# First phase of an attention and feed-forward block: second half of a projection by pairs of row tiles, V and weights ahead of K's DMA transposes

## The chip, the cores and the metric

One core of one Trainium2 chip. The metric is device time in microseconds (us) of one execution. The record also has each execution's mean granted TensorE clock (1.000 is full speed). In the profile's lines PE is TensorE, PEld its weight loads, DVE VectorE, ACT ScalarE, POOL GpSimd and SPq the DMA issues of SyncE.

## The reference

```python
x   = A_x                                             # (1, 2048, 1024), bf16
mod = silu(c) @ w_mod                                 # six vectors sa, ca, ga, sb, cb, gb
h   = layernorm(x) * (1 + ca) + sa
q   = h @ wq                                          # 32 heads of 128
p   = softmax(q @ k.T / sqrt(128)); o = p @ v         # 4 kv heads, the last 512 keys
x   = x + ga * (o @ wo)
h   = layernorm(x) * (1 + cb) + sb
x   = x + gb * ((silu(h @ w_gate) * (h @ w_up)) @ w_down)   # inner size 3584
```

## The kernel before

The kernel walks through four chunks of 512 rows. In the steady part each step is one head: scores (`s_ps`), the query product of a head seven steps ahead (`q_ps`), and the weighted sum (`o_ps`). Only the first phase, up to about 36 us, is touched. There the layernorm of the first chunk is multiplied by `1 + ca` (`hs`), and the query products of heads 0 to 6 ("D") are accumulated over eight row tiles `dt` of the weights, which come in four DMAs `wq8` of two row tiles each. The shift `sa` is added later as a bias: `sa_mm` computes it in one-column products, `sh_mm` multiplies it with the weights.

The DMA queue (all issued by SyncE, in this order):

```python
    for tt in range(QT):            # four 128-row tiles of x
        load_x(tt)
    for half in range(DH):
        load_wm(1, half)            # w_mod columns of ca
        load_wq8(2 * half)          # heads 0-7, two row tiles each
        load_wq8(2 * half + 1)
    load_wm(0, 0)                   # w_mod columns of sa, first half
    h10 = hpool.tile([P, DT, TCW], BF16, name="hT", tag="hT")
    load_wm(0, 1)
    kT = blkB("kT", [P, Hkv, W])
    for kv in range(Hkv):           # K, transposed on the way in
        pin(nc.sync.dma_start_transpose(
            out=kT[:, kv, :], in_=A_k_cache[0, kv, k0:k0 + W, :]), "dma")
    ...
    for kv in range(Hkv):
        load(v_sb[:, kv, :, 0:Dh], v_v[:, kv])
    load_wq(0, 2)                   # third group's weights: heads 8-11, two DMAs of 512 KB
```

The part of PE's order that is touched (program order is kept here):

```python
    def q0(g, dts, src=None):       # head g, row tiles dts: one 128x512 product each
        for dt in dts:
            nc.tensor.matmul(q0_ps[g], lhsT=w0(g, dt), rhs=..., start=(dt == 0), stop=(dt == DT - 1))
    ...                             # first half of D: row tiles 0 to 3 of all seven heads
    for g in range(3):
        q0(g, range(4, DT))
    q0(3, (4, 5))
    sa_mm(0, (0, 1))
    q0(3, (6, 7))
    sa_mm(0, (2, 3))
    sa_out(0)                       # DVE: PSUM -> sa, sa_bf
    q0(4, (4, 5))
    sh_mm(0, range(4))
    q0(4, (6, 7))
    sh_mm(0, range(4, H0))
    for dt in range(4):
        ln_mod(("h1", 0), dt, ca1, sa)                                   # DVE
    nc.vector.tensor_copy(out=bias_q, in_=one_ps[:, 1, 0:H0])            # DVE
    q0(5, (4, 5))
    sa_mm(1, (0, 1))                # writes one_ps: waits for that copy
    q0(5, (6, 7))
    sa_mm(1, (2, 3))
    sa_out(1)
    q0(6, (4, 5))
    sh_mm(1, range(H0))             # waits for sa_bf
    q0(6, (6, 7))
    ...
    nc.vector.tensor_tensor(out=bias_q, in0=one_ps[:, 2, 0:H0], in1=bias_q, op=ALU.add)
    q0_ps[H0] = mm("q_ps")          # takes one_ps's bank: waits for that addition
    q0(H0, range(DT), h10)          # head 7
```

After this come head 0's scores (they need K of kv head 0, "K0"), head 8's query product (the third group's weights) and head 0's weighted sum (V of kv head 0, "V0").

Of the kernel before, what the change touches and what calls it, by code (L numbers as in the profile page):

```python
# [11 lines left out]
BF16 = mybir.dt.bfloat16  # L12
# [576 lines left out]
def fast_path(ctx, tc, flag, A_x, A_k_cache, A_v_cache, A_wq, A_wo, B_x, B_w_gate, B_w_up,  # L589
# [4 lines left out]
    P = 128  # L594
    _, S, D = A_x.shape
    _, Hkv, Sk, Dh = A_k_cache.shape
# [9 lines left out]
    DT = D // P  # L606
    FT = F // P
    WT = W // P
# [20 lines left out]
    const = ctx.enter_context(tc.tile_pool(name="const", bufs=1))  # L629
# [13 lines left out]
    def blkB(name, shape, dt=BF16):  # L643
        return pb_.tile(shape, dt, name=name, tag="B")
# [4 lines left out]
    def mm(name, shape=(P, 512), dt=FP32):  # L649
        return psp.tile(list(shape), dt, name=name, tag="mm", bufs=4)  # L650
# [9 lines left out]
    def pin(ins, what="steps"):  # L660
        return tc.keep_in_program_order(ins) if stage[what] else ins

    def fetch(out, in_):
        pin(nc.sync.dma_start(out=out, in_=in_), "dma")  # L664

    def load(out, in_):
        with nc.allow_non_contiguous_dma(reason="weight slice"):
            fetch(out=out, in_=in_)
# [32 lines left out]
    def load_wq(cc, hg, parts=(0, 1)):  # L701
        for i in parts:
            t = blkB("wq", [P, 4, 512])
            load(t, wq_v[:, 4 * i:4 * i + 4, hg * 512:(hg + 1) * 512])
            wq_tiles[(cc, hg, i)] = t

    H0 = 7
# [14 lines left out]
    h10 = hpool.tile([P, DT, TCW], BF16, name="hT", tag="hT")  # L722
    load_wm(0, 1)
    kT = blkB("kT", [P, Hkv, W])
    for kv in range(Hkv):
        pin(nc.sync.dma_start_transpose(  # L726
            out=kT[:, kv, :], in_=A_k_cache[0, kv, k0:k0 + W, :]), "dma")
    VN = Dh + 2
    v_sb = const.tile([P, Hkv, WT, Dh + 32], BF16, name="v_sb")
    for kv in range(Hkv):  # L730
        load(v_sb[:, kv, :, 0:Dh], v_v[:, kv])
    load_wq(0, 2)

    ones_bf = const.tile([P, P], BF16, name="ones_bf")
    nc.vector.memset(ones_bf, 1.0)
# [24 lines left out]
    nc.gpsimd.tensor_tensor(out=sil_r, in0=c_r, in1=ec, op=ALU.mult)  # L760
    nc.gpsimd.memset(v_sb[:, :, :, Dh:VN], 1.0)
    siluc = const.tile([P, DT], BF16, name="siluc")
# [229 lines left out]
    def h_scale(dt, src=None, on_act=False):  # L992
        src = h10[:, dt, :] if src is None else src
        if on_act:
            nc.scalar.activation(out=hs[dt // 4][:, dt % 4, :], in_=src, func=ACT.Identity,
                                 scale=ca1[:, dt:dt + 1])
        else:
            nc.vector.tensor_scalar(out=hs[dt // 4][:, dt % 4, :], in0=src,
                                    scalar1=ca1[:, dt:dt + 1], scalar2=None, op0=ALU.mult)
# [15 lines left out]
    def w0(g, dt):  # L1015
        return wq8[dt // 2][:, dt % 2, g * P:(g + 1) * P]

    def q0(g, dts, src=None):
        for dt in dts:
            nc.tensor.matmul(q0_ps[g], lhsT=w0(g, dt),  # L1020
                             rhs=hs[dt // 4][:, dt % 4, :] if src is None else src[:, dt, :],
                             start=(dt == 0), stop=(dt == DT - 1))
# [4 lines left out]
    def sh_mm(half, heads):  # L1027
        for g in heads:
            for i in range(4):
                dt = 4 * half + i  # L1030
                nc.tensor.matmul(one_ps[:, 1 + half, g:g + 1], lhsT=w0(g, dt),
                                 rhs=sa_bf[:, dt:dt + 1], start=(i == 0), stop=(i == 3))

    def sa_mm(half, tiles):
        for i in tiles:
            c = 4 * half + i
            for dt in range(DT):
                nc.tensor.matmul(one_ps[:, 0, c:c + 1],
                                 lhsT=wm_tiles[(0, half)][:, dt, i * P:(i + 1) * P],
                                 rhs=siluc[:, dt:dt + 1], start=(dt == 0), stop=(dt == DT - 1))  # L1040

    def sa_out(half):
        c = slice(4 * half, 4 * half + 4)
        nc.vector.tensor_copy(out=sa[:, c], in_=one_ps[:, 0, c])
        nc.vector.tensor_copy(out=sa_bf[:, c], in_=sa[:, c])
# [4 lines left out]
    for i in range(2):  # L1050
# [4 lines left out]
        if i == 0:  # L1055
            mod_cols(1, 1, ca1, True)
            for dt in range(4, DT):
                h_scale(dt)
    for g in range(3):
        q0(g, range(4, DT))  # L1060

    q0(3, (4, 5))
    sa_mm(0, (0, 1))
    q0(3, (6, 7))
    sa_mm(0, (2, 3))
    sa_out(0)
    q0(4, (4, 5))
    sh_mm(0, range(4))
    q0(4, (6, 7))
    sh_mm(0, range(4, H0))  # L1070
    for dt in range(4):
        ln_mod(("h1", 0), dt, ca1, sa)
    nc.vector.tensor_copy(out=bias_q, in_=one_ps[:, 1, 0:H0])
    q0(5, (4, 5))
    sa_mm(1, (0, 1))
    q0(5, (6, 7))
    sa_mm(1, (2, 3))
    sa_out(1)
    q0(6, (4, 5))
    sh_mm(1, range(H0))  # L1080
    q0(6, (6, 7))
    for dt in (4, 5):
        ln_mod(("h1", 0), dt, ca1, sa)
    for dt in (6, 7):
# [119 lines left out]
    def emit_o(g):  # L1204
# [4 lines left out]
        for t in range(QT):  # L1209
            if o_slot["n"] == 0:  # L1210
                o_slot["ps"] = mm("o_ps", (P, SLOTS, VN))
            s_ = o_slot["n"]
            for j in range(WT):
                nc.tensor.matmul(o_slot["ps"][:, s_, :], lhsT=pT[g][:, j, t * P:(t + 1) * P],  # L1214
                                 rhs=v_sb[:, kv, j, 0:VN], start=(j == 0),
                                 stop=(j == WT - 1))
# [146 lines left out]
    for k in range(NU + 1):  # L1363
        if k % 4 >= 2 and 4 * (k // 4) + 12 < NU:
            g = 4 * (k // 4) + 12
# [49 lines left out]
def kernel(tc, *args):  # L1415
    nc = tc.nc
    with tc.tile_pool(name="guard", bufs=1) as gp:
        flag = gp.tile([1, 1], I32, name="flag")
        over = fast_path(tc, flag, *args)
        with tc.If(over > 0):  # L1420
            general_path(tc, *args)
# [30 lines left out]
```

## Time and profile before

| | before |
|---|---|
| median, 6 executions | 1274.25 us (1273.68 to 1274.90) |
| span of the profiled execution | 1272.4 us, mean clock 1.000 |
| first score product starts | 30.48 us |
| first product of the weighted sum (`o_ps`) starts | 35.42 us |
| from there to the end | 1236.96 us |

Busy time by engine, kernel before: busy us, share of the span, instructions.

```profile
PE 1255.9 (99%) x7445; PEld 640.0 (50%) x7587; DVE 610.0 (48%) x1335; ACT 335.6 (26%) x440; POOL 1.3 (0%) x10
```

TensorE bounds the kernel, and from 36 us to the end the list of waits of PE is empty. What is left is the start. PE's waits from 0 to 60 us, kernel before (us in total, times, longest us):

```profile
PE warm_ps L746 <- DVE warm_w L737: 1.6, 1, 1.6
PE q_ps L1171 <- DMA wq<-in_A_wq_dram: 1.1, 2, 0.8
PE q_ps L1020 <- DMA wq<-in_A_wq_dram: 0.5, 1, 0.5
PE h_ps L948 <- DVE xn L852: 0.5, 2, 0.3
PE one_ps L1038 <- DMA wm<-in_w_mod_dram: 0.2, 1, 0.2
```

`q_ps L1171` is head 8's query product: it waited 1.1 us for the third group's weights. `q_ps L1020` is D: it waited 0.5 us for the last `wq8`. The timeline of PE, kernel before (start us, duration us, engine, line, operation, count, idle before and what ended it):

```profile
19.39 2.76 PE L1020 MATMUL q_ps<-hs,wq 128*128 128x512 bf16 x12 [0.54 <-DMA wq<-in_A_wq_dram]
22.39 0.55 PE L1038 MATMUL one_ps<-siluc,wm 128*128 128x1 bf16 x16 [0.24 <-DMA wm<-in_w_mod_dram]
...
25.79 0.54 PE L1038 MATMUL one_ps<-siluc,wm 128*128 128x1 bf16 x16
26.41 0.38 PE L1020 MATMUL q_ps<-hs,wq 128*128 128x512 bf16 x1
26.63 0.54 PE L1038 MATMUL one_ps<-siluc,wm 128*128 128x1 bf16 x16
27.03 0.59 PE L1020 MATMUL q_ps<-hs,wq 128*128 128x512 bf16 x2
27.62 0.84 PE L1031 MATMUL one_ps<-sa_bf,wq 128*128 128x1 bf16 x28
28.33 0.59 PE L1020 MATMUL q_ps<-hs,wq 128*128 128x512 bf16 x2
28.75 1.89 PE L1020 MATMUL q_ps<-hT,wq 128*128 128x512 bf16 x7
30.48 1.03 PE L1182 MATMUL s_ps<-qT,kT 128*128 128x512 bf16 x4
32.30 0.82 PE L1171 MATMUL q_ps<-hT,wq 128*128 128x512 bf16 x3 [0.79 <-DMA wq<-in_A_wq_dram]
...
34.12 0.39 PE L1171 MATMUL q_ps<-hT,wq 128*128 128x512 bf16 x1 [0.35 <-DMA wq<-in_A_wq_dram]
...
35.42 1.07 PE L1214 MATMUL o_ps<-v_sb,pT 128*128 128x130 bf16 x16
```

The durations of neighbours overlap (the pair at 28.33 us is shown with 0.59 us, the next product starts at 28.75), so the starts are what to read. A few records are missing (the pair before 26.63 shows as x1, head 7's eight products as x7). The DMA queue behind it, SyncE's timeline, kernel before:

```profile
14.83 10.23 SPq L726 DMA_TRANSPOSE kT<-in_A_k_cache_dram  x4
25.11 2.92 SPq L664 DMA_DIRECT2D v_sb<-in_A_v_cache_dram  x4
28.07 1.55 SPq L664 DMA_DIRECT2D wq<-in_A_wq_dram  x2
```

The issues of the four transposes and of V stand in front, so the weights are only issued at 28.07. And the table by stretch, kernel before; the column after POOL is the granted clock:

```profile
26.00:29.40 3.40, 3.27 (x65) 2.17 (x64) 1.84 (x7) 1.94 (x3) 0.00 (x0) 1.00 0.92 196
29.40:32.80 3.40, 2.61 (x13) 1.05 (x12) 3.28 (x6) 2.42 (x4) 0.00 (x0) 1.00 0.85 277
```

### The profile page before, as it was taken

Reading aid. Unit: us, or ns where it says so; the run is one execution under the profiler, and the core shown is the slowest. Engines: PE = TensorE matmul, PEld = TensorE weight load, DVE = VectorE, ACT = ScalarE, POOL = GpSimd, SP = SyncE. Lnnn points to the kernel's source line nnn. Section 1 sums busy time; section 2 is a strip of 40 time slices with the busy share of each in tenths; the row PEclk is TensorE's granted clock in tenths of the full one; section 3 lists DMA queues with packets and bytes.
Section 4 is the critical chain, followed back from the end, with each engine's and each line's share of the span. In section 5 each row is a group of like instructions: output and inputs, shape, how many; then the busy total and the mean of one; then the engine's idle time right before and its main releaser. Section 6 shows DMA issues by size and latency. Waiting matters only on the chain.

```text
span 1272.4 us, 18018 instructions
## 1 busy us (share of the span) xinstructions
PE 1255.9 (99%) x7445; PEld 640.0 (50%) x7587; DVE 610.0 (48%) x1335; ACT 335.6 (26%) x440; POOL 1.3 (0%) x10
## 2 busy tenths in 40 slices
PE   8999999999999999999999999999999999999998
PEld 4555555555555555555554444444444444444444
DVE  5666658885778665567564631321122112221122
ACT  3643334343333433334341111011100111011100
POOL 0000000000000000000000000000000000000000
PEclk9999999999999999999999999999999999999999
DMA  9897656778556655454575379336633565425702
GB/s 286 202 252 172 181 141 147 187 161 214 130 141 171 152 134 157 113 154 108 125 199 149 129 222 258 95 93 210 211 110 112 167 211 184 157 91 169 245 18 68
DMA packets 306844, 204.46 MB, mean 161 GB/s; under 512 B 145601, under 2 KB 303297, under 8 KB 306754
## 3 DMA queue, kind: packets, MB, share of 16 engines
q1 hardware_dynamic: 301842, 199.03, 57.0%
q10 hardware_dynamic: 4912, 4.20, 1.0%
q8 instruction: 61, 1.00, 0.3%
q14 instruction: 29, 0.24, 0.1%
HBM read 165.94 MB, written 4.21 MB: 134 GB/s over the span
## 4 chain that ended last, share of the span: by engine, by line
PE 95%; SPq 2%; DVE 1%; issue 1%; DMA 0%
PE gu_ps L1328 30%; PE a_ps L1246 17%; PE q_ps L1171 16%; PE d_ps L1348 15%; PE o_ps L1214 9%; PE s_ps L1182 8%; SPq L664 1%; SPq L726 1%; DMA wq<-in_A_wq_dram 0%; DVE junk L1105 0%; DVE st L833 0%; DVE junk L804 0%; DVE oq L1201 0%; DVE qT L934 0%; DVE f L1259 0%
## 5 line engine op out<-in xcount | busy, mean ns | idle before, releaser
L1184 ACT ACTIVATE pT<-s_ps 128x1024 bf16<-128x1024 f32 x256 | 249.3, 1020 | 346.1 <-PE s_ps L1182 225.5
L1246 PE MATMUL a_ps<-wo,oT 128*128 128x512 bf16 x987 | 240.1, 380 | 1.9
L1171 PE MATMUL q_ps<-hT,wq 128*128 128x512 bf16 x958 | 227.1, 380 | 1.2 <-DMA wq<-in_A_wq_dram 1.1
L1334 DVE TENSOR_TENSOR guT<-gu_ps,sg 128x512 bf16<-128x512 f32 x112 | 77.5, 692 | 287.0 <-ACT sg L1333 287.0
L1328 PE MATMUL gu_ps<-hT,wg 128*128 128x512 bf16 x879 | 210.1, 380 | 0.9
L1333 ACT ACTIVATE sg<-gu_ps 128x512 bf16<-128x512 f32 x112 | 66.9, 597 | 488.7 <-PE gu_ps L1328 417.4
L1348 PE MATMUL d_ps<-wd,guT 128*128 128x512 bf16 (+2 forms) x935 | 193.3, 367 | 0.9
L1328 PE MATMUL gu_ps<-hT,wu 128*128 128x512 bf16 x656 | 161.7, 379 | 0.8
L1246 PEld LDWEIGHTS <-oT 128*128 128x128 bf16 x1024 | 100.0, 98 | 120.7
L934 DVE CAST qT<-q_ps 128x512 bf16<-128x512 f32 x121 | 83.6, 691 | 153.0 <-PE q_ps L1171 150.6
L1171 PEld LDWEIGHTS <-wq 128*128 128x128 bf16 x960 | 93.7, 98 | 114.9 <-DMA wq<-in_A_wq_dram 2.1
L1348 PEld LDWEIGHTS <-guT 128*128 128x128 bf16 x952 | 90.7, 98 | 103.1
L1214 PEld LDWEIGHTS <-pT 128*128 128x128 bf16 x2048 | 126.5, 98 | 30.6 <-issue 0.4
L1328 PEld LDWEIGHTS <-wg 128*128 128x128 bf16 x896 | 87.5, 98 | 105.6
L1214 PE MATMUL o_ps<-v_sb,pT 128*128 128x130 bf16 x2048 | 137.1, 221 | 0.2
L1182 PE MATMUL s_ps<-qT,kT 128*128 128x512 bf16 x469 | 129.4, 380 | 2.3
L1328 PEld LDWEIGHTS <-wu 128*128 128x128 bf16 x672 | 65.7, 98 | 79.4
L1201 DVE TENSOR_TENSOR oq<-o_ps,rl 128x256 bf16<-128x256 f32 (+2 forms) x256 | 100.4, 419 | 3.9
L1352 DVE TENSOR_TENSOR f<-d_ps,gb_bc 128x512 f32<-128x512 f32 (+2 forms) x34 | 22.4, 660 | 140.7 <-PE d_ps L1348 122.1
L1182 PEld LDWEIGHTS <-kT 128*128 128x128 bf16 x512 | 44.9, 98 | 30.8
L1254 DVE TENSOR_TENSOR acc<-a_ps,acc 128x512 f32<-128x512 f32 x64 | 44.0, 688 | 32.6 <-PE a_ps L1246 32.6
L1328 PE MATMUL gu_ps<-hT,v_sb 128*128 128x512 bf16 x219 | 56.8, 380 | 0.3
(97 smaller groups left out, 424.3 us busy)
## 6 DMA issues: line engine op xcount, KB each, us to landing
wq<-in_A_wq_dram SPq DMA_DIRECT2D x64, 512.0 KB
wo<-in_A_wo_dram SPq DMA_DIRECT2D x64, 512.0 KB
wg<-in_B_w_gate_dram SPq DMA_DIRECT2D x56, 512.0 KB
wd<-in_B_w_down_dram SPq DMA_DIRECT2D x56, 512.0 KB
wu<-in_B_w_up_dram SPq DMA_DIRECT2D x42, 512.0 KB
v_sb<-in_B_w_up_dram SPq DMA_DIRECT2D x14, 512.0 KB
x<-in_A_x_dram SPq DMA_DIRECT2D x16, 256.0 KB
wm<-in_w_mod_dram SPq DMA_DIRECT2D x4, 1024.0 KB
```

The source lines that it names most:

```text
L934: nc.vector.tensor_copy(out=t, in_=q_ps)
L1171: nc.tensor.matmul(q_ps, lhsT=w, rhs=hT[("h1", cc)][:, dt, :], start=(dt == 0), stop=(dt == DT - 1))
L1182: nc.tensor.matmul(s_ps[:, i, :], lhsT=kT[:, kv, j * P:(j + 1) * P], rhs=qT[g], start=True, stop=True)
L1184: nc.scalar.activation(out=p[:, 2 * jj:2 * jj + 2, :], in_=s_ps, func=ACT.Exp, scale=scale)
L1201: nc.vector.tensor_tensor(out=dst, in0=ps[:, s0:s0 + cnt, 0:Dh], in1=sc, op=ALU.mult)
L1214: nc.tensor.matmul(o_slot["ps"][:, s_, :], lhsT=pT[g][:, j, t * P:(t + 1) * P], rhs=v_sb[:, kv, j, 0:VN], start=(j == 0), stop=(j == WT - 1))
L1246: nc.tensor.matmul(a_ps, lhsT=oT[(cc, 2 * q + i)][:, hh % 4, t * P:(t + 1) * P], rhs=wo_tiles[(cc, q, dh, i)][:, hh % 4, :], start=(hh == ...
L1254: nc.vector.tensor_tensor(out=acc[(cc, t)][:, dsl], in0=a_ps, in1=acc[(cc, t)][:, dsl], op=ALU.add)
L1328: nc.tensor.matmul(ps[:, n, :], lhsT=gu_w[(cc, fg, nm, dt // 4)][:, dt % 4, fi * P:(fi + 1) * P], rhs=hT[("h2", cc)][:, dt, :], start=(dt ...
L1333: nc.scalar.activation(out=g, in_=ps[:, 0, :], func=ACT.Silu)
L1334: nc.vector.tensor_tensor(out=guT[(cc, fg)][:, fi, :], in0=ps[:, 1, :], in1=g, op=ALU.mult)
L1348: nc.tensor.matmul(d_ps, lhsT=guT[(cc, f // 4)][:, f % 4, t * P:(t + 1) * P], rhs=wd_tiles[(cc, dh, f // 4)][:, f % 4, c0:c0 + w], start=( ...
```

## The change

Two intents. First, no product of D should wait for the last `wq8`: all heads take the third `wq8` (row tiles 4, 5) before any takes the fourth (6, 7). Second, head 8 should not wait for its weights: V0 and the third group's weights are issued ahead of K. No instruction is added or removed.

```diff
     load_wm(0, 1)
     kT = blkB("kT", [P, Hkv, W])
-    for kv in range(Hkv):
+
+    def load_kT(kv):
         pin(nc.sync.dma_start_transpose(
             out=kT[:, kv, :], in_=A_k_cache[0, kv, k0:k0 + W, :]), "dma")
-    ...
-    for kv in range(Hkv):
+
+    def load_v(kv):
         load(v_sb[:, kv, :, 0:Dh], v_v[:, kv])
+
+    load_v(0)
     load_wq(0, 2)
+    load_kT(0)
+    for kv in range(1, Hkv):
+        load_kT(kv)
+    for kv in range(1, Hkv):
+        load_v(kv)
@@
-    for g in range(3):
-        q0(g, range(4, DT))
-
-    q0(3, (4, 5))
+    for g in range(H0):
+        q0(g, (4, 5))
+
+    q0(0, (6, 7))
+    q0(1, (6, 7))
     sa_mm(0, (0, 1))
-    q0(3, (6, 7))
+    q0(2, (6, 7))
     sa_mm(0, (2, 3))
     sa_out(0)
-    q0(4, (4, 5))
+    q0(3, (6, 7))
     sh_mm(0, range(4))
     q0(4, (6, 7))
     sh_mm(0, range(4, H0))
     ...
-    q0(5, (4, 5))
     sa_mm(1, (0, 1))
     q0(5, (6, 7))
     sa_mm(1, (2, 3))
     sa_out(1)
-    q0(6, (4, 5))
+    q0(6, (6, 7))
     sh_mm(1, range(H0))
-    q0(6, (6, 7))
```

More of the change, by code (lines that the diff above doesn't have):

```diff
@@ L724, in fast_path @@
     kT = blkB("kT", [P, Hkv, W])
-    for kv in range(Hkv):
+    VN = Dh + 2
+    v_sb = const.tile([P, Hkv, WT, Dh + 32], BF16, name="v_sb")
+    def load_kT(kv):
         pin(nc.sync.dma_start_transpose(
             out=kT[:, kv, :], in_=A_k_cache[0, kv, k0:k0 + W, :]), "dma")
-    VN = Dh + 2
-    v_sb = const.tile([P, Hkv, WT, Dh + 32], BF16, name="v_sb")
-    for kv in range(Hkv):
+    def load_v(kv):
         load(v_sb[:, kv, :, 0:Dh], v_v[:, kv])
+    load_v(0)
     load_wq(0, 2)
+    load_kT(0)
[3 more added lines that the diff above has]
+        load_v(kv)
     ones_bf = const.tile([P, P], BF16, name="ones_bf")
```

## The prediction

> **What bounds the kernel.** TensorE. The busy table gives PE 1255.9 us of the 1272.4 us span (99%), granted clock 1.00; the list of waits shows none of PE from 36 us to the end. A steady step takes 3.49 us on the timeline. The change touches only the first 36 us and is worth what PE's chain there gets shorter; 2% is out of reach. Upper bound, from the list of waits to 60 us: PE idle for DMA 1.1 us (head 8's query product, third group's weights: 0.79 and 0.35), 0.5 us (second half of D, last wq8 tile), 0.2 us (sa product, its w_mod half): 1.9 us.
>
> **What the change does.** Nothing is added or removed; only PE's order (28 products of D's second half) and the DMA queue's order change.
>
> 1. *D by pairs of row tiles.* Before, PE runs 8+2 products from 16.54 us, waits for the last wq8 tile (last engine 19.34), resumes at 19.39, and waits until 22.39 for the w_mod half of sa that lands at 22.34. After, 14 products need only the third tile (there at 18.0): the 0.5 us wait goes, and 18 instead of 14 of the 28 are done by 22.15. But sa still starts at 22.39: its DMA is ahead of every moved one. The four products won (4 x 0.215 = 0.86 us) are missing later, where they filled waits for DVE:
>  - sa's second half waits until DVE has copied bias_q (25.54 to 25.71, behind 1.38 us of scalings). Before, q0(5)'s pair filled that and it started at 25.79; after, idle about 0.4 us, start 25.75.
>  - Head 7's product takes one_ps's bank and waits for the bias_q addition (28.50 to 28.67). Before, q0(6)'s last pair filled that; it started at 28.75. After, idle about 0.35 us, start 28.7.
>  So the reordering gives 0 to 0.1 us.
>
> 2. *V0 and weights ahead of K.* [...] the trace's completion counts agree (25.24 w_mod, 25.7 K0, 27.2 K3, then V, weights 32.25 and 34.07). Moved ahead, the weights land at 27 to 28.7: the 0.79 and 0.35 us waits go. ACT's exponentials (1.94 us a head) then gate the second head's scores: from first score product to first o product I count 3.7 us instead of 4.94 (30.48 to 35.42). Gain about 1.2 us, kept to the end.
>
> 3. *Cost.* 1.18 MB now precedes K0. At the 0.36 MB/us of the window table (before 20 us), plus about 0.6 us for V0's small packets, that is 3.5 us: K0 lands at about 29.2 (estimate), needed at 30.3. If one DMA engine lags by 1 us, as several landings show, it just misses; I subtract 0.15 us on average. Other K and V parts are needed later.
>
> **Predicted:** gain 1.1 us, 1273.0 us (1271.9 to 1274.2). Faster by over 2%: 0.5%; within 2%: 99%; slower: 0.5%.
>
> **What would show it.** Right: no PE wait on weights near 32 to 34 us; first o product at 34.2 us, not 35.4; first score product still at 30.2 to 30.5; new PE gaps of about 0.4 us near 25.4 and 28.4, released by DVE; sa still at 22.4. Wrong on 1: first score product by 29.7. Wrong on 3: PE waiting for K's transpose before it.
>
> **What would make it wrong.** K0 after 30.3 us (each us late is a us lost); sa's w_mod landing at another time; the spread of runs, 1.2 us over three, as large as the effect.

In the trace of before the loads landed in the order of their issue (last of 16 engines: w_mod 25.24 us, K0 25.71, V0 29.07, the weights 32.25 and 34.07; K3's last but one 27.2). 0 to 0.1 us of point 1 and 1.2 of point 2, less 0.15 of point 3, are the 1.1 us predicted. In point 3, the 0.6 us for V0 is the author's estimate; in the trace of before the four V loads came 0.63 us apart on average (first of 16 engines: 27.67 to 29.56 us). The lag of one engine is measured there too: 16 engines had landed the third `wq8` at 18.00 us, 15 of them at 17.02.

## More of the kernel before

A wide product here is one of 512 columns, against the one-column products of `sa_mm` and `sh_mm`.

## The result, and the profile after

The changed kernel took 1274.53 us (median of 6, 1273.60 to 1275.43) against 1274.25 before; the ratio is 1.0002, with a 95% interval of 0.9989 to 1.0015. A ratio is the mean time of one kernel's runs over that of the other's of the same rounds, so it is not quite the ratio of the medians quoted. The predicted 1273.0 (a gain of 1.1 us) is outside the measurement: nothing was gained. An effect of 1 us is 0.08%, smaller than the interval of any single comparison here, so what follows rests on the traces, on counts of executions, and on differences between kernels that shared the same runs of before.

PE's waits from 0 to 60 us, changed kernel (its lines from L735 on are 8 or 9 higher):

```profile
PE warm_ps L755 <- DVE warm_w L746: 1.6, 1, 1.6
PE h_ps L957 <- DVE xn L861: 1.5, 2, 1.4
PE q_ps L1029 <- DVE bias_q L1094: 0.3, 1, 0.3
PE one_ps L1047 <- DVE bias_q L1083: 0.3, 1, 0.3
```

The waits for DMA are gone, all 1.9 us of them (0.2 us of it, for sa's w_mod half, only because PE came later: that DMA landed at 22.00 us, and sa started at 22.86). The two waits for DVE that the prediction foresaw are there. One wait grew that the change does not touch: the first transposes of x (`h_ps`) waited 1.4 us, because x landed later in this execution. The timeline of PE, changed kernel:

```profile
17.25 5.77 PE L1029 MATMUL q_ps<-hs,wq 128*128 128x512 bf16 x26
22.86 0.54 PE L1047 MATMUL one_ps<-siluc,wm 128*128 128x1 bf16 x16
...
26.22 0.54 PE L1047 MATMUL one_ps<-siluc,wm 128*128 128x1 bf16 x16 [0.26 <-DVE bias_q L1083]
26.62 0.59 PE L1029 MATMUL q_ps<-hs,wq 128*128 128x512 bf16 x2
27.05 0.54 PE L1047 MATMUL one_ps<-siluc,wm 128*128 128x1 bf16 x16
27.45 0.59 PE L1029 MATMUL q_ps<-hs,wq 128*128 128x512 bf16 x2
28.05 0.84 PE L1040 MATMUL one_ps<-sa_bf,wq 128*128 128x1 bf16 x28
29.14 3.33 PE L1029 MATMUL q_ps<-hT,wq 128*128 128x512 bf16 x8 [0.26 <-DVE bias_q L1094]
32.26 1.32 PE L1190 MATMUL s_ps<-qT,kT 128*128 128x512 bf16 x4
...
36.25 1.07 PE L1222 MATMUL o_ps<-v_sb,pT 128*128 128x130 bf16 x16
```

The phase ends at 36.25 us instead of 35.42, 0.83 us later, and from there to the end both kernels take the same (1236.89 and 1236.96 us). So the whole difference is in these lines. The line to stop at is 29.14: head 7's eight products took 3.33 us, where seven took 1.89 before. The table by stretch, changed kernel, says why:

```profile
26.00:29.40 3.40, 2.92 (x66) 2.09 (x66) 1.58 (x7) 1.51 (x3) 0.00 (x0) 1.00 1.96 159
29.40:32.80 3.40, 3.40 (x10) 1.23 (x9) 3.40 (x6) 1.15 (x3) 0.00 (x0) 0.50 1.01 187
```

For one stretch TensorE was granted half its clock. PE looks fully busy there (3.40 of 3.40 us, 10 products) and does less (an execution of this order at clock 1.00, r6 below, has 15 products in 3.38 us): the busy share hides a slow clock. The trace's own records put the stretch at 29.43 to 32.84 us, 3.41 us long. By my estimate from these two numbers, half of that, 1.7 us, is lost if TensorE has work all through it; r6 measured 1.70 us.

The moved DMAs, SyncE's timeline, changed kernel:

```profile
14.90 4.10 SPq L664 DMA_DIRECT2D v_sb<-in_A_v_cache_dram  x1
19.04 2.92 SPq L664 DMA_DIRECT2D wq<-in_A_wq_dram  x2
22.01 6.64 SPq L729 DMA_TRANSPOSE kT<-in_A_k_cache_dram  x4
```

By the completion counts in the trace (last of 16 engines), the weights landed at 27.10 and 28.50 us instead of 32.25 and 34.07, and K0 at 30.38 instead of 25.71.

Three theories, then. **C (clock)**: the changed order leaves so few wide products between the sparse one-column ones that the clock is halved in part of the executions, for 1.7 us. **K (K's landing)**: K0, now behind 1.18 MB, takes the gain. **J or N (start, chance)**: the start jitters with the landing of the first x rows, and the rest is chance; the halved clock has nothing to do with the change.

### The profile page after: what moved, and what is told of

Read it like the earlier page. It is cut to its first block, busy times and chain, and to the rows that moved or that the text cites. A ratio compares the mean times of both kernels' runs of the same rounds, so it can differ in the third digit from the quotient of the medians.

```text
span 1273.1 us, 18160 instructions
## 1 busy us (share of the span) xinstructions
PE 1264.5 (99%) x7587; PEld 641.5 (50%) x7587; DVE 610.1 (48%) x1335; ACT 335.6 (26%) x440; POOL 1.3 (0%) x10
## 4 chain that ended last, share of the span: by engine, by line
PE 97%; DVE 2%; DMA 0%; SPq 0%; issue 0%
PE gu_ps L1336 30%; PE a_ps L1254 17%; PE q_ps L1179 16%; PE d_ps L1356 15%; PE o_ps L1222 9%; PE s_ps L1190 8%; PE q_ps L1029 1%; DVE st L842 0%; DMA x<-in_A_x_dram 0%; DVE junk L1113 0%; DVE junk L813 0%; DVE oq L1209 0%; DVE qT L943 0%; DVE f L1267 0%; DVE f L1266 0%; DVE x L1269 0%
```

## The experiments

r1 to r4 shared one chip and nine runs of before, r5 to r8 a second chip and nine, r9 and r10 a third and nine. "Difference" is the mean of five executions less the mean of those nine; its standard error, from the two spreads, is 0.2 to 0.45 us. By the formal interval of the ratio (about 0.0013 either way) all but r7 hold 1. All results were correct.

| run | mean us | difference | mean clock of the five executions |
|---|---|---|---|
| r1 the change again | 1274.07 | -0.32 | 0.998 0.999 0.999 1.000 0.998 |
| r2 queue order only | 1273.60 | -0.80 | 0.999 0.999 0.999 1.000 0.999 |
| r3 pair order only | 1274.41 | +0.02 | 1.000 0.998 0.999 0.999 0.999 |
| r4 pairs held back | 1273.29 | -1.11 | 0.999 0.999 0.999 1.000 0.999 |
| r5 before, with tail | 1274.99 | +0.51 | 1.000 1.000 1.000 1.000 1.000 |
| r6 change, with tail | 1275.21 | +0.73 | 1.000 1.000 0.999 0.999 0.999 |
| r7 sparser, with tail | 1276.38 | +1.90 | 0.999 0.999 0.997 0.999 0.997 |
| r8 held back, K0 first | 1273.19 | -1.29 | 0.999 1.000 0.999 0.999 1.000 |
| r9 held back, with tail | 1273.99 | -0.17 | 1.000 1.000 1.000 1.000 1.000 |
| r10 early pairs, K0 first | 1272.96 | -1.20 | 1.000 0.999 1.000 0.999 1.000 |

### r1: the change again

No edit.

> The changed kernel, unaltered, for more executions. Theory C (clock): the pair order leaves TensorE so thinly used between about 26 and 29.4 us that in part of the executions the granted clock is halved for one stretch of 3.4 us, at head 7's product and the first scores, which costs about 1.6 us; the rest of the executions gain about 1.1 us or a little less. Then the executions fall in two groups, mean clock 0.998 (slow group) and 0.999 to 1.000, about 1.4 us apart, with at least a fifth in each. Theory K (K's landing): K0 lands at about 30.4 us in every execution and takes the gain by itself; then no difference between groups of clock. Theory N (nothing gained, only the start jitters): executions without the halved clock are on average no faster than those of before.

Measured: 0.3 us faster than before, executions from 1273.26 to 1275.02. Two of five had clock 0.998, the slowest two (1275.02 and 1274.49); the other three averaged 1273.62. That looks as C has it. But this run's profile corrected me on the reading of the clock: its halved stretch was at 8.55 to 11.96 us, after a wait of 2.0 us for x, where the change does nothing. A mean clock of an execution can't tell that stretch from one at 29 us. In its trace the products of that stretch are longer (eight `h_ps` 0.93 us, against 0.62 in the kernel before). Worse, TensorE is idle at the end (4.8 us in before's profile, from 1267.54 to 1272.38), and the clock is recorded as halved there too, where no product is left to slow (in before's profile from 1272.37 us on, in r2's from 1269.97), so 0.999 can mean a harmless tail. Nor do these 0.998 show C, since the one that was profiled came from the start. This called for the tail of r5 to r7.

### r2: only the queue's order

Against before; PE's order is not touched:

```diff
-    for kv in range(Hkv):
-        pin(nc.sync.dma_start_transpose(... kT[:, kv, :] ...), "dma")
-    for kv in range(Hkv):
-        load(v_sb[:, kv, :, 0:Dh], v_v[:, kv])
+    load_v(0)
     load_wq(0, 2)
+    load_kT(0)
+    for kv in range(1, Hkv):
+        load_kT(kv)
+    for kv in range(1, Hkv):
+        load_v(kv)
```

> Only the DMA queue's order of the change; PE's order as before. Theory C: the gain is all here, because the stretch from 26 to 29.4 us stays as dense as before: the waits for the third group's weights are gone, first o product 1.0 to 1.3 us sooner after the first x row tile's product than before, mean clock 1.000 or 0.9995 in nearly all executions, 0.7 to 1.2 us faster than before. Theory K: K0 lands at 30.2 to 30.5 and PE waits 0.3 us or more for it; faster by at most 0.5 us. Theory N: within 0.3 us of before.

Measured: 0.80 us faster; no execution at 0.998. In its trace K0 landed at 30.84 us and PE waited for it; the first score product started at 30.88, and the first `o_ps` 3.71 us later. PE's waits, r2:

```profile
PE s_ps L1191 <- DMA kT<-in_A_k_cache_dram: 0.3, 1, 0.3
PE one_ps L1047 <- DMA wm<-in_w_mod_dram: 0.2, 1, 0.2
```

Both C and K get a part: the queue's order alone gains most of what was predicted, and K0 takes 0.3 us of it, as in my third step, where I had estimated 29.2 us for K0 and subtracted 0.15. K expected at most 0.5 us of gain, so it is not the main cause.

### r3: only the pair order

Against before; the queue is not touched, and the rest of the change's second hunk follows in the same way:

```diff
-    for g in range(3):
-        q0(g, range(4, DT))
-
-    q0(3, (4, 5))
+    for g in range(H0):
+        q0(g, (4, 5))
+
+    q0(0, (6, 7))
+    q0(1, (6, 7))
     sa_mm(0, (0, 1))
 ...
```

> Only PE's pair order of the change; the DMA queue as before. By my recorded step 1 the first score product starts within 0.1 us of before's, and the waits for the third group's weights (0.8 and 0.35 us) stay or grow, so without a halved clock equal to before within 0.2 us. Theory C: a part of the executions, as large as in the changed kernel, has the halved clock (mean 0.998) and is slower by 0.5 to 1.6 us, part of it hidden by the wait for weights; on average 0.3 to 0.8 us slower than before. Rival: the halved clock comes from the queue's order or from chance; then it is as rare here as in before.

Measured: no difference (+0.02 us), one of five at 0.998. C had said 0.3 to 0.8 us slower: a miss in size. The trace shows room for hiding: the third group's weights land at 32.20 and 33.62 us here and head 8 still waits for them (its weight loads waited 1.0 us, in two waits), so time lost before about 32 us is partly made up by a shorter wait. That this is the reason is argued, not shown.

### r4: two pairs held back

Against the change:

```diff
-    for g in range(H0):
+    for g in (0, 1, 2, 3, 4, 6):
         q0(g, (4, 5))
@@
     nc.vector.tensor_copy(out=bias_q, in_=one_ps[:, 1, 0:H0])
+    q0(5, (4, 5))
     sa_mm(1, (0, 1))
@@
-    q0(6, (6, 7))
     sh_mm(1, range(H0))
+    q0(6, (6, 7))
```

> The changed kernel, but q0(5)'s first pair is held back to where PE waits for the copy of bias_q, and q0(6)'s last pair to where it waits for the bias addition: the same products, the gaps filled as before. Theory C: the halved clock is gone or as rare as in the queue-order-only kernel, 0.7 to 1.2 us faster than before, no PE wait of 0.26 us for DVE. If the clock is halved as often as in the changed kernel, the gaps are not its cause. My step 1: the first score product starts at the same time as in the changed kernel's executions of full clock, within 0.1 us, since the held-back pairs only fill waits.

Measured: 1.11 us faster, and the slowest of its five executions (1273.53) was faster than the fastest of before's nine (1273.76). It differs from the change (-0.32 in the same rounds) only in where two pairs of products stand. The timeline of PE, r4:

```profile
27.52 0.84 PE L1040 MATMUL one_ps<-sa_bf,wq 128*128 128x1 bf16 x28 [0.46 <-DVE sa_bf L1054]
28.22 0.59 PE L1029 MATMUL q_ps<-hs,wq 128*128 128x512 bf16 x2
28.65 1.89 PE L1029 MATMUL q_ps<-hT,wq 128*128 128x512 bf16 x8
30.80 1.04 PE L1191 MATMUL s_ps<-qT,kT 128*128 128x512 bf16 x4 [0.26 <-DMA kT<-in_A_k_cache_dram]
```

The waits for bias_q are filled, one of 0.46 us for sa_bf is new (I had overlooked that q0(6)'s first pair stood there), and head 7's eight products take 1.89 us. K0 is waited for here as well. The expectation that the first score product starts within 0.1 us of the change's at full clock can't be read: it started at 30.80, in r6 at 31.11, after different starts of x.

### r5, r6, r7: counting halved stretches

To make the mean clock readable, 20 dummy products keep TensorE busy to the end, so only halved stretches at the start should count: by the 1.7 us estimated above one stretch is 1.7 of 1272 us, so 0.999; two are 0.997. r5 is before with this tail, r6 the change with it, and r7 a sparser version of the change with it:

```diff
+    tail_ps = mm("tail_ps")
+    for _ in range(20):
+        nc.tensor.matmul(tail_ps, lhsT=ones_bf, rhs=warm_w, start=True, stop=True)
     assert not tasks
@@ r7 only, against the change
     q0(1, (6, 7))
+    q0(5, (6, 7))
+    q0(6, (6, 7))
     sa_mm(0, (0, 1))
@@
     sa_mm(1, (0, 1))
-    q0(5, (6, 7))
     sa_mm(1, (2, 3))
     sa_out(1)
-    q0(6, (6, 7))
```

> The kernel before, with 20 dummy products behind its last one (they fill TensorE's idle 4.3 us at the end, so that the mean granted clock of an execution counts only stretches of half clock at the start: 1.000 none, 0.999 one, 0.997 two). An instrument, not a candidate; its time should be that of before within 0.3 us. Theory C (clock halved because of the sparse stretch left by the pair order): at most one of six executions at 0.999. Theory J (the start of the first products jitters by up to 1.7 us with the landing of the x rows; in before the landing of the third group's weights at about 34 us hides that, in the changed kernel nothing does, and the clock is chance): as many half-clock executions as in the changed kernel; its times spread by less than those of the changed kernel.

Measured: no halved stretch in five, the idle end included (all five 1.000; that end is 4.8 us in before's trace, not 4.3). The tail itself costs about 0.5 us (more than the 0.3 I had allowed; standard error 0.33), so r5, r6, r7 and r9 are compared with each other. One of the five took 1276.04 us at full clock, 1.0 us over the next, which nothing on record explains (see r6 for what 1.000 can miss); without it r5's mean is 1274.72.

> The changed kernel with the same 20 dummy products at its end. Theory C: two to four of six executions at 0.999 (5 of the 11 so far showed 0.998, with an idle tail), these at least 0.8 us slower than the ones at 1.000, and the ones at 1.000 about 1.0 us faster than before. Theory J: no more half-clock executions than in the kernel before with this tail; times at 1.000 spread over more than 1 us.

Measured: three of five executions had a halved stretch. They took 1275.73, 1275.81 and 1276.12 us; the two at full clock took 1274.01 and 1274.36. The groups do not overlap and their means are 1.70 us apart, which is half of 3.41 us. At full clock the change is 0.8 us faster than r5 (1274.19, of two executions, against 1274.99; 0.5 us without r5's slowest). The profiled execution was one at full clock: head 7's eight products took 1.89 us. But its trace holds no clock record at all, nor does r9's, so a mean of 1.000 says only that no half clock was recorded. The table by stretch, r6:

```profile
26.00:29.40 3.40, 2.81 (x66) 2.05 (x65) 1.51 (x7) 1.44 (x3) 0.00 (x0) 1.00 2.10 202
29.40:32.80 3.40, 3.38 (x15) 1.29 (x14) 3.40 (x6) 2.27 (x5) 0.00 (x0) 1.00 0.99 99
```

There the first score product started at 31.11 and the first `o_ps` at 34.82, 3.71 us apart as predicted.

> The changed kernel with the last pairs of q0(5) and q0(6) moved up in front of the first sa product, so that no wide product runs between about 26 and 29.3 us; with the same tail. The two pairs delay the sa product by about 0.6 us. Theory C: more half-clock executions than in the changed kernel, at least four of six, and at least 1 us slower on average than the changed kernel. If the halved clock has another cause than the sparse stretch: no more of them than in the changed kernel, and about 0.6 us slower.

Measured: all five had a halved stretch, two of them two (where the second lay is not recorded); 1.17 us slower than r6. The sa product started at 23.72 instead of 22.93 in r6 (0.8 us later, 0.6 expected). The table by stretch, r7, whose halved stretch the trace records at 29.69 to 33.10 us:

```profile
26.00:29.40 3.40, 2.60 (x78) 2.16 (x75) 1.97 (x9) 1.09 (x2) 0.00 (x0) 1.00 1.45 203
29.40:32.80 3.40, 3.01 (x7) 1.12 (x8) 3.37 (x6) 1.57 (x3) 0.00 (x0) 0.54 1.46 146
```

Fewer wide products between 26 and 29.4 us, more halved stretches: 0 of 5, 3 of 5, 5 of 5. J (as many in r5 as in r6) falls, by r5 against r7 above all: 0 against 3 of five alone could be chance.

### r8: K0 first

Against r4:

```diff
-    load_v(0)
-    load_wq(0, 2)
     load_kT(0)
+    load_wq(0, 2)
+    load_v(0)
```

> A candidate: pairs held back as in r4, and in the DMA queue K0 first, then the third group's weights, then V0, the rest of K and V. In r2 and r4 PE waited 0.26 us for K0, which landed at 30.8. Theory K (K0's landing after the moved weights takes part of the gain): K0 lands at about 25.7, the wait is gone, weights land at 29 to 30.5 without a new wait, and the kernel is 0.2 to 0.4 us faster than r4's distance to before, so 1.3 to 1.5 us faster than before. If the weights now arrive after about 31.5 us, a wait for them comes back and the gain is that of r4 or less.

Measured: K0 landed at 25.12 us, the weights at 26.59 and 28.16, no wait for any of them in the list; 1.29 us faster than before against r4's 1.11. The wait of 0.26 us is gone for certain; that it shows as 0.2 us in the time is within the error of the two differences.

### r9: the cure, counted

r4's kernel with r5's tail, no other edit.

> r4's kernel (the change, with q0(5)'s first and q0(6)'s last pair held back) with the 20 dummy products at its end, so that its mean clock counts half-clock stretches as in r5, r6 and r7 (0 of 5, 3 of 5, 5 of 5 executions had one). Theory C: none or one of five at 0.999; mean time 0.9 to 1.3 us under that of r5 relative to before, so 0.4 to 0.8 us faster than before (the tail itself cost 0.5 us in r5). If the halved clock came with the moved DMAs or with the pair order as such, two to four of five at 0.999 and no gain.

Measured: none of five with a halved stretch. Between the kernels of r6 (three of five) and r9 nothing differs but the place of two pairs, though r9 ran on another chip; the moved DMAs are the same. Zero against three of five alone could again be chance; with it go r1 and r4 on one chip (two of five at 0.998, one of them from the start, against none) and r8 (none). It was 0.17 us faster than its own before, less than the 0.4 expected, and 0.68 us better than r5's difference (which has an error of 0.4 us with it).

### r10: only the early pairs

Against before, beside r8's queue:

```diff
-    for g in range(3):
-        q0(g, range(4, DT))
-
-    q0(3, (4, 5))
+    for g in range(4):
+        q0(g, (4, 5))
+    for g in range(3):
+        q0(g, (6, 7))
     sa_mm(0, (0, 1))
```

> A candidate: PE's order as before from the first sa product on; only in the seven pairs ahead of it the third tile's four come first, then the last tile's three. DMA queue as in r8 (K0, third group's weights, V0, the rest). By theory C and K nothing thins out the stretch from 26 to 29 us and K0 is not waited for: 1.2 to 1.5 us faster than before, as r8 (1.29), spread under 1 us. If what held r8 back is PE's idle 0.46 us for sa_bf, which q0(6)'s first pair fills here, it is up to 0.1 us better, not more, because that wait ends with DVE either way.

Measured: 1.20 us faster, all five executions (1272.55 to 1273.37) under the fastest of before's nine (1273.78). Everything from the first sa product on stands as before. All of PE's waits up to 60 us, r10:

```profile
PE warm_ps L755 <- DVE warm_w L746: 1.6, 1, 1.6
PE h_ps L957 <- DVE xn L861: 0.9, 2, 0.7
```

No wait for a load of weights or K and none for DVE after the first transposes. Its first `o_ps` started at 33.75 us. On the means it beats both kernels (the formal interval, 0.9978 to 1.0005, still holds 1); r8 is its equal within the errors.

## Why the prediction was wrong

- **The step that failed is the end of point 1, "So the reordering gives 0 to 0.1 us."** The gaps were predicted where they came (0.26 and 0.26 us measured, 0.4 and 0.35 predicted), and I took them as free, since the products won elsewhere paid for them. They are not free. With the same queue order, the change is 0.78 us slower than r4 (1274.07 and 1273.29) and, with the tail, 0.9 us behind r9 (+0.73 and -0.17). In r6 all of it is in executions where the clock is halved once: 1.70 us each, three of five.
- **A second part of point 1 failed, and no halved clock is needed for it:** "But sa still starts at 22.39: its DMA is ahead of every moved one." With four more products in front of it, sa started later than its DMA had landed: at 22.86 in the changed kernel (landed 22.00) and at 22.93 in r6 (22.54). From `mod_ps` (L782) to sa it took 6.41 us in both, and 5.55 in r10, which leaves these four behind sa. So at full clock, where PE and not the DMA sets sa's start, the order loses up to 0.86 us there and wins back 0.07 us by head 7 (6.28 us from sa to head 7 in r6, 6.35 in r10). How much of r10's lead in time over the change comes from this and how much from K0 was not tested apart.
- **The sum then closes, within the errors.** Gain predicted without the clock: 1.1 us; measured where the clock stays whole: 0.8 us (r6 at full clock against r5), 0.8 (r2), 1.1 (r4). Loss: three fifths of 1.7 us, about 1.0 (the share is only roughly known: three of five). Left: about nothing, and the changed kernel measured +0.21 and -0.32 us in its two sets.
- **What the halving depends on.** The traces show granted shares of 0.5 and 1.0 alone, a halved stretch of 3.41 us (29.43 to 32.84), and in the changed kernel's trace 23.89 us, seven times 3.413, from the first record of full clock (5.54) to the halving. The halved clock at the idle end fits the same step (23.89 / 7 us): it comes 363.0 steps after full clock returned in the changed kernel (1239.04 us) and 371.0 steps after the first record of full clock in the kernel before (1266.35 us). From this I estimate that the clock is set in such steps. Counted so, a step starts at 26.51 us in the trace of before, 26.02 in the changed kernel's, 25.61 in r1's, 25.34 in r3's and 24.07 in r4's, so it starts elsewhere in each execution. That the work in one step decides the clock of the next is my assumption; it would explain why a sparse stretch is caught in part of the executions, and no run tests it by itself. Before the result I had looked for long idle times only; the longest idle in or next to the sparse stretch is 0.26 us in the changed kernel. In the step before the halving, 26.02 to 29.43 us, the timeline above shows four wide products and the first of head 7's, with a third of its second, among 60 one-column ones. In the kernel before, the 3.4 us from 26.0 on held three pairs (at 26.41, 27.03 and 28.33 us) and three products of head 7, nine wide ones with the missing records, and r5 had no halving in five.
- **How many wide products went with a kept clock.** Each trace that holds clock records shows where its own steps lay, if they are counted by 3.413 us from its first record of full clock, and on the assumption above that brackets the need. With six whole wide products among 60 to 63 one-column ones the clock stayed whole in the step that followed in r1 (step 25.61 to 29.03), r3 (25.34 to 28.75; pairs from 25.40, 26.93 and 27.76) and r4 (24.07 to 27.48; pairs from 24.53, 25.26 and 26.09); after five and a third it was halved in the changed kernel, after about one in r7 (26.27 to 29.69). PE's busy time does not sort these: a step of the changed kernel (5.54 to 8.95) was followed by a whole clock with PE busy for only 2.03 us (seven wide products started in it and eight of 128 columns), and its step from 26.02 us by a halved one with PE busy for 2.95 us. From the start times in the traces an estimate follows, on the same assumption and if a step may start anywhere with equal chance: 23 to 31% of the positions leave too few wide products in the change's order (r1's trace), 89 to 97% in r7's, 12 to 21% in r4's and none in that of before (r2's trace, in which no record of these pairs is missing).
- **Point 2 was right**: the 0.79 and 0.35 us waits went, and from the first score to the first `o_ps` product took 3.70 or 3.71 us in r1, r2, r4 and r6 (3.7 predicted, 4.94 before).
- **Point 3 was right in kind, small in size**: the estimate for K0 was 29.2 us; it landed at 29.27 to 29.49 in r1 and r7 and at 30.38 to 31.06 in the others. Where it came late, a pause of 1.9 to 2.0 us lay between the last weights and K0; in r1 and r7 the pause lay between K0 and K1 (29.49 to 31.35 us in r1), and with K0 first, in r10, between the weights and V0 (28.30 to 30.27), neither of them a transpose. Its cause is open. PE waited 0.26 us in r2 and r4, against 0.15 us subtracted.
- **The profile of before was a favourable execution**: its first transpose of x began at 7.15 us, those of the other runs at 6.96 to 8.40. A late start is partly swallowed by before's own waits for weights, and less so once those are gone. No run here separates this part; it may be why r2 shows 0.8 us and not 1.1.

Open: whether holding two pairs back (r4, r8, r9) removes the halving or only makes it rarer; by the estimate above 0 of 5 would be no surprise either way, and r10's order, which keeps that of before from sa on, is the safer one. The bracket of five and a third to six wide products rests on few steps and on the assumption that one step decides the next, and of the halved executions only two were profiled with the stretch behind the sparse part (the changed kernel's and r7's); the others are counted by their mean clock. r1's profiled halving at 8.55 us belongs to the start, which all kernels share. Of the changed kernel's executions without a tail, 5 of 11 had 0.998 (one of the nine of before in r1's rounds had it too), and those of 0.999 can't be told apart.

## What to carry to other kernels

Before moving wide products away from a stretch of small ones to fill an earlier wait, count what stays behind. In these traces a step of 3.41 us with six wide products was followed by a whole clock and one with five and a third by a halved one; the gaps were of 0.26 us, cost nothing on the dependency chain by my count, and yet the executions with a halved stretch took 1.70 us longer in r6. Check too whether the work moved forward delays what stands behind it, once the engine and no longer the DMA sets that start (here by up to 0.86 us). Read the granted clock by stretch and execution by execution, because a halved clock makes PE look busier (3.40 of 3.40 us at clock 0.50 here), and the mean over a long kernel hides it (0.998). When moving a load ahead in a queue, put what is needed first (K0, one head's share) first, and only then the larger load: K0 landed at 25.12 us in r8, and at 30.38 us behind V0 and the weights in the changed kernel.
